# Start of a fused adaLN, attention and GEGLU kernel: scales of the first chain on VectorE, second half's LayerNorm tiles on GpSimd

## The chip, the cores and the metric

The kernel runs on one core of one Trainium2 chip. The metric is the device time of one execution in microseconds (us). Engines are named as in the profile: PE is TensorE (PEld its weight loads), DVE is VectorE, ACT is ScalarE, POOL is GpSimd, SP is SyncE, whose queue issues nearly all transfers.

## The reference

One block of a transformer on 2048 tokens of width 512, in f32. All shift, scale and gate columns come from one small product of `silu(c)` with `w_mod`.

```python
mod = (_silu(c) @ w_mod).reshape(c.shape[0], 6, 1, -1)
sa, ca, ga, sb, cb, gb = (mod[:, 0], mod[:, 1], mod[:, 2], mod[:, 3], mod[:, 4], mod[:, 5])
h = _layernorm(x, axis=-1) * (1 + ca) + sa
x = x + ga * _A_ref(h, A_k_cache, A_v_cache, A_wq, A_wo)
h = _layernorm(x, axis=-1) * (1 + cb) + sb
x = x + gb * _B_ref(h, B_w_gate, B_w_up, B_w_down)
...
# _A_ref: 32 query heads on 8 key/value heads of 128, over the last 512 positions of the cache
q = (x @ wq)
scores = jnp.einsum("bhqd,bhkd->bhqk", q, k) * (Dh ** -0.5)
p = _softmax(scores, axis=-1)
o = jnp.einsum("bhqk,bhkd->bhqd", p, v)
...
# _B_ref
return (_gelu(x @ w_gate) * (x @ w_up)) @ w_down
```

## The kernel before, in words

Every large product is made of three f16 products: each f32 operand is scaled and split into a high half (rounded to f16) and a low half (the rest), and high times high, high times low and low times high are summed in PSUM. The scales keep the halves within f16's range; they are bounds worked out on the chip from norms and maxima (`wsc` for wq, `ksc` for k, `qsc` for q, `ma` for the normalised input; `kmax` and `lw` are norms, `lu`, `lt`, `lr` steps between). Later query projections and the feed-forward part use seven products in the place of eight.

Tokens go in blocks of 512 (four tiles of 128 rows, `QT`), two blocks to a half. The main loop counts steps `t`: each step makes the scores `ps` of one 128-row tile for one head, their maximum `nm` (DVE, `peak`), the exponential `ee` (ACT, `expo`), the probabilities `p` in two halves (ACT and DVE), a transpose of them by DMA (`pt`), and takes a few groups of other matmuls from a list (projections `pq`, `po`, `py`). The order on every engine is written out by hand: functions put under `at(key, ...)` run at that step, and each engine executes its instructions strictly in that order. A wait of one instruction holds back all behind it on its engine.

`begin()` is what runs ahead of step 0. This is the part that the change rewrites:

- The first four x tiles are normalised (`na`): statistics on DVE, the power -1/2 on POOL, the normalisation `xn` on DVE (tiles 0 and 1) and on ACT (tiles 2 and 3).
- The shift column `cols[:,0]` is made by 32 recorded f32 matmuls (`early_cols`, tile `mps`, L1031); the scale column `cols[:,1]` by four multiply-and-sum passes on DVE (`mod_col`, L138). `mod_scale` takes the larger of both over all partitions (`mm`, turned by PE into `pst`, reduced to `mg`) and scales the columns.
- `ln_out(qb, dt)` makes the 512 columns of block `qb` for one quarter `dt` of the width. `turn` transposes four tiles on PE into `pln`; `affine` applies scale and shift to an f32 copy `hf`, which is also stored to DRAM; `direct` does the same to the high half (tile `b` in the profile); `low` subtracts the two.
- `high_w`, `low_w` split wq (`w`), `k0[3]` splits k, `q_first` makes the first query projection `pq`, and `q_post` splits that into `qt`. `warm` and `fill` are matmuls on dummy data.

The second block's four tiles (`nb`, rows 512 to 1023, tile `xb` in the profile) have their statistics and normalisation in steps 0 to 2. Tile 0 goes through ACT (`centre`, `scale`), tiles 1 to 3 through DVE:

```python
at(0, nb[0][2], nb[0][3], nb[1][0], nb[1][1], nb[2][0], nb[2][1])
at(1, nb[1][2], nb[3][0], nb[3][1], nb[2][2])
...
at(2, nb[3][2], *[o[0] for o in o1])
```

The transposes of `xb` (`o1[dt][0]`) stand in PE's order behind the scores of step 2 and ahead of those of step 3: tiles 0 and 1, four `fill`, tile 2, four `fill`, tile 3 and with it the 12 transposes of the other three quarters.

Of the kernel before, what the change touches and what calls it, by code (L numbers as in the profile page):

```python
# [18 lines left out]
P = 128  # L19
# [46 lines left out]
def block_kernel(ctx: ExitStack, tc: tile.TileContext, x, kT, v, wq, wo, wg, wu, wd, cT, wc, wm, out):  # L66
# [47 lines left out]
    nc.gpsimd.memset(nhalf, -0.5)  # L114
    half_ = const.tile([P, 1], F32, name="half_")
    nc.gpsimd.memset(half_, 0.5)
    ones = const.tile([P, 1], BF16, name="ones")
    nc.gpsimd.memset(ones, 1.0)
    junk = const.tile([P, 512], F16, name="junk")
# [59 lines left out]
    def col(name, i=0):  # L179
        return ST[name][:, i:i + 1]  # L180
# [10 lines left out]
    def absmax(out, src):  # L191
        nc.vector.tensor_reduce(out, src, axis=AX.X, op=ALU.max, apply_absolute_value=True)

    def everywhere(out, m, n, fold=True):
        ps = bank("acc", "pst", NACC)
        for i in range(n):
            nc.tensor.transpose(ps[:, i * P:(i + 1) * P], m[:, i:i + 1].to_broadcast([P, P]), ident)
        src = ps[:, :n * P] if fold else ps[:, :n * P].rearrange("p (n q) -> p n q", n=n)
        nc.vector.tensor_reduce(out, src, axis=AX.X, op=ALU.max)
# [3 lines left out]
        absmax(m, cols[:, j:j + 2, :])  # L203
        return m

    def mod_scale(j, name, const_, m=None, mid=nop, between=nop):
        m, g, s = m or mod_max(j), little("mg", 2, 1), little("ms", 1, 1)
        everywhere(g, m, 2, False)
        mid()
        nc.vector.tensor_tensor(s, g[:, 0:1], g[:, 1:2], op=ALU.add)  # L210
# [10 lines left out]
    def sums(m, n):  # L221
        ps = bank("acc", "pst", NACC)
        nc.tensor.matmul(ps[:, 0:n], ones.to_broadcast([P, P]), m[:, 0:n], start=True, stop=True)
        return ps

# [179 lines left out]
    def ln_first(i, act=False):  # L405
        st = {}

        def norm():
            if i < QT:
                xn[i] = tmp("xn")  # L410
                nc.vector.tensor_scalar(xn[i], acc[i], st["mv"][:, 0:1], st["rs"], op0=ALU.subtract, op1=ALU.mult)
            else:
                xn[i] = xn["b"][:, i - QT, :]
                nc.vector.tensor_scalar(xn[i], acc[i], st["mv"][:, 0:1], st["rs"], op0=ALU.subtract, op1=ALU.mult)

        def centre():
            if i < QT:
                xn[i] = tmp("xn")
            else:
                xn["b"] = pool.tile([P, QT, 512], F32, tag="pt", name="xb", bufs=NPT)  # L420
                xn[i] = xn["b"][:, 0, :]
            nc.scalar.activation(xn[i], acc[i], AF.Identity, bias=st["nm"], scale=1.0)

        def scale():
            nc.scalar.activation(xn[i], xn[i], AF.Copy, scale=st["rs"])

        pre = (lambda: ln_stat(acc[i], st, act), lambda: ln_power(st))
        return pre + ((centre, scale) if act else (norm,))

    def ln_out(qb, dt):  # L430
# [1 line left out]
        p = dt % 2  # L432
        st = {}

        def turn():
            st["ps"] = bank("acc", "pln", NACC)
            for i in range(QT):
                if qb and dt == 0 and i > 1:
                    fill(4)
                nc.tensor.transpose(st["ps"][:, i * P:(i + 1) * P], xn[qb * QT + i][:, dt * P:(dt + 1) * P], ident)  # L440
# [9 lines left out]
        def direct():  # L450
            nc.scalar.activation(block(0, name)[:, p, :], st["ps"], AF.Identity, scale=cols[:, 1, dt:dt + 1], bias=cols[:, 0, dt:dt + 1])

        def low(eng=nc.vector):
            t = block(0, name)
# [569 lines left out]
    wct = [pool.tile([P, 4, 512], F32, tag="pt", name="wct", bufs=NPT) for _ in range(2)]  # L1024

    def early_load(j, dt):
        dma(wct[j][:, dt, :], wc[1, :, dt, :] if j else wm[0, dt])

    def early_cols(ps, dt, w=None):
        for kt in range(KT):  # L1030
# [19 lines left out]

    gps = {}
    na = [ln_first(i, i >= 2) for i in range(QT)]
    nb = [ln_first(QT + i, i == 0) for i in range(QT)]
    o0 = [ln_out(0, dt) for dt in range(KT)]
    SET[0] = [get_w(0), get_w(1)]

# [5 lines left out]

    def q_first(warm):
        ps = bank("acc", "pq", NACC)
        for term, (a, b) in enumerate(((0, 0), (1, 0), (0, 2))):
            for kt in range(KT):
                w, m, p = SET[0][0], BK[0, ("b11", "b21")[kt // 2]], kt % 2
                nc.tensor.matmul(ps, w[:, a, kt * P:(kt + 1) * P], m[:, b + p, :], start=term + kt == 0, stop=term == 2 and kt == KT - 1)
            if term == 0:
                warm(3)  # L1070
        q_post(0, ps)

    def begin():
        now[0] = -1
        for i in range(QT):
            na[i][0]()
            na[i][1]()
        na[2][2]()
        na[3][2]()
        na[0][2]()  # L1080
        na[1][2]()
        na[2][3]()
        na[3][3]()
        block(0, "y")
        for name in ("b11", "b21", "b22", "t3", "t2", "t4", "t1"):
            block(0, name)
        mps = bank("s", "mps", 2)
        wps = bank("s", "warm", 2)

        def warm(n):  # L1090
            for _ in range(n):
                nc.tensor.matmul(wps, junk[:, 0:P], junk, start=True, stop=True)

        for dt in range(KT):
# [5 lines left out]
        pair_stat(0, m, 1)  # L1100
        k0[1]()
        ts(cols[:, 1, :], cols[:, 1, :], 1.0, None, ALU.add)
        ts(cols[:, 0, :], mps[:, 0:KT], 1.0, None, ALU.mult)
        pst = {}

        def mid():
            o0[0][0]()
            pst["w"] = sums(m["m"], 2)
            o0[1][0]()
            pst["k"] = sums(k0[4]["m"], 1)  # L1110
            o0[2][0]()
            o0[3][0]()

        mod_scale(0, "ma", SCALE * TOP13 * TOP13, mod_max(0), mid)
        w = w_first(m["m"], pst["w"])
        o0[0][1](False)
        inv_k = k0[2](False, pst["k"])
        nc.vector.reciprocal(col("wsc", 0), w)
        inv_t, last = w_spread(0, m["m"], w)
        o0[0][3]()  # L1120
        high_w(0)
        for n in range(1, KT):
            o0[n][1](False)
            o0[n][3]()
            if n == 1:
                o0[0][2](nc.gpsimd)
            if n == 2:
                inv_k()
                inv_t()
                last()  # L1130
        warm(4)
        low_w(0)
        o0[1][2]()
        o0[2][2](nc.gpsimd)
# [708 lines left out]
```

## Time and profile before

| what | value |
|---|---|
| median of 3 runs | 1729.52 us (1729.38 to 1730.45) |
| the profiled execution: own time, span of its instructions | 1731.43 us, 1729.6 us |
| busy share of the span: PE, DVE, ACT, POOL | 99%, 82%, 73%, 63% |
| PE busy from 100 to 120 us | 20.00 of 20.00 us |
| PE busy from 0 to 10, 10 to 20, 20 to 24 us | 4.84, 8.86, 2.91 us |
| first maximum of scores (`nm`) begins | 26.06 us |

The profiled execution took 1.9 us longer than the median of the timed runs, and its span is 1.8 us shorter than its own time. Times in the views count from the start of the span; in a row of the timeline the first number is the start, the second the duration (for `x4`, of the four together), and the square bracket gives the idle time ahead of it on its engine and what ended that.

### The profile page before, as it was taken

Reading aid. Unit: us, or ns where it says so; the run is one execution under the profiler, and the core shown is the slowest. Engines: PE = TensorE matmul, PEld = TensorE weight load, DVE = VectorE, ACT = ScalarE, POOL = GpSimd, SP = SyncE. Lnnn points to the kernel's source line nnn. Section 1 sums busy time; section 2 is a strip of 40 time slices with the busy share of each in tenths; the row PEclk is TensorE's granted clock in tenths of the full one; section 3 lists DMA queues with packets and bytes.
Section 4 is the critical chain, followed back from the end, with each engine's and each line's share of the span. In section 5 each row is a group of like instructions: output and inputs, shape, how many; then the busy total and the mean of one; then the engine's idle time right before and its main releaser. Section 6 shows DMA issues by size and latency. Waiting matters only on the chain.

```text
span 1729.6 us, 26339 instructions
## 1 busy us (share of the span) xinstructions
PE 1709.0 (99%) x8012; PEld 786.6 (45%) x8012; DVE 1426.7 (82%) x2476; ACT 1254.7 (73%) x2819; POOL 1090.0 (63%) x1328
## 2 busy tenths in 40 slices
PE   7999999999999999999999999999999999999999
PEld 5444444444444444444444444444444444444444
DVE  7888898888889899888788888888896788676666
ACT  6988788888888877888777877787785354455442
POOL 4879778777788984655665755757760345735424
PEclk9999999999999999999999999999999999999999
DMA  7999999999999998999999999999997556365353
GB/s 235 222 206 209 215 215 204 225 205 219 210 231 218 210 208 183 212 209 228 202 228 214 215 230 209 203 219 225 218 230 166 157 153 195 120 164 174 96 160 102
DMA packets 693454, 343.51 MB, mean 199 GB/s; under 512 B 579136, under 2 KB 602688, under 8 KB 693312
## 3 DMA queue, kind: packets, MB, share of 16 engines
q1 hardware_dynamic: 693024, 341.30, 85.7%
q8 instruction: 63, 1.03, 0.2%
q14 instruction: 79, 0.65, 0.1%
q10 hardware_dynamic: 288, 0.52, 0.1%
HBM read 137.50 MB, written 63.70 MB: 116 GB/s over the span
## 4 chain that ended last, share of the span: by engine, by line
PE 88%; DVE 4%; ACT 3%; DMA 2%; POOL 1%; issue 1%; SPq 0%; POOLq 0%; ACTq 0%; DVEq 0%
PE py L91 19%; PE po L91 17%; PE ps L91 17%; PE fa L91 8%; PE qa L91 8%; PE fc L91 4%; PE qc L91 4%; PE ya L91 3%; PE fb L91 2%; PE qb L91 2%; PE yc L91 2%; DMA pt<-p 1%; DVE p L1016 1%; ACT ee L999 1%; DVE nm L990 1%
## 5 line engine op out<-in xcount | busy, mean ns | idle before, releaser
L999 ACT ACTIVATE ee<-ps,nm 128x512 f32<-128x512 f32 x512 | 349.7, 683 | 185.6 <-DVE nm L990 180.3
L1016 DVE SCALAR_TENSOR_TENSOR p<-ee,rr,p 128x512 f16<-128x512 f32 x512 | 458.3, 895 | 8.1 <-ACT p L1011 7.6
L990 DVE TENSOR_REDUCE nm<-ps 128x1 f32<-128x512 f32 x512 | 350.3, 684 | 97.5 <-PE ps L91 95.2
L91 PE MATMUL ps<-k,qt 128*128 128x512 f16 x1536 | 414.9, 379 | 4.9 <-ACT ee L999 3.5
L1011 ACT ACTIVATE p<-ee,rr 128x512 f16<-128x512 f32 x512 | 364.0, 711 | 20.1 <-DVE rr L1007 11.3
L91 PE MATMUL po<-pt,v 128*128 128x512 f16 x1536 | 372.9, 379 | 2.6 <-DMA pt<-p 0.9
L91 PE MATMUL py<-wo,ot 128*128 128x512 f16 x1536 | 371.3, 379 | 0.0
L91 PEld LDWEIGHTS <-w 128*128 128x128 f16 x2184 | 213.5, 98 | 258.6 <-issue 0.9
L91 PEld LDWEIGHTS <-v 128*128 128x128 f16 x1536 | 150.0, 98 | 184.8 <-issue 2.8
L91 PEld LDWEIGHTS <-ot 128*128 128x128 f16 x1536 | 150.3, 98 | 181.3
L91 PEld LDWEIGHTS <-qt 128*128 128x128 f16 x1536 | 145.7, 98 | 176.4 <-issue 4.6
L1320 POOL TENSOR_TENSOR fg<-fg 128x512 f32<-128x512 f32 x48 | 62.9, 1310 | 134.6 <-DVE fg L1294 131.8
L748 DVE SCALAR_TENSOR_TENSOR ot<-po,ot 128x512 f16<-128x512 f32 x128 | 87.9, 687 | 39.2 <-ACT ot L747 38.7
L1304 ACT ACTIVATE at<-fg 128x512 f16<-128x512 f32 x92 | 56.3, 625 | 80.2 <-DVE fg L1294 60.7
L999 ACT ACTIVATION_READ_ACCUMULATOR ee<-ps,nm 128x1 f32 x512 | 100.1, 196 | 0.0
L960 DVE SCALAR_TENSOR_TENSOR acc<-py,ysc,acc 128x512 f32<-128x512 f32 x128 | 94.7, 740 | 5.3 <-PE py L91 5.3
L91 PE MATMUL qa<-t,w 128*128 128x512 f16 x348 | 84.9, 379 | 0.0
L236 POOL TENSOR_TENSOR lw<-lw,half__86 128x1 f32<-128x1 f32 x39 | 24.9, 639 | 94.7 <-DVE lw L186 94.6
L91 PE MATMUL fa<-t,w 128*128 128x512 f16 x336 | 81.6, 379 | 0.1
L747 ACT ACTIVATE ot<-po 128x512 f16<-128x512 f32 x128 | 73.9, 577 | 5.0 <-PE po L91 5.0
L403 POOL TENSOR_TENSOR rs<-rs,nhalf 128x1 f32<-128x1 f32 x32 | 18.7, 584 | 92.7 <-DVE rs L397 89.7
L91 PEld LDWEIGHTS <-wo 128*128 128x128 f16 x504 | 49.3, 98 | 59.6 <-issue 0.3
(243 smaller groups left out, 2813.8 us busy)
## 6 DMA issues: line engine op xcount, KB each, us to landing
w<-kept SPq DMA_DIRECT2D x123, 256.0 KB, 3.3
wo<-kept SPq DMA_DIRECT2D x72, 256.0 KB, 3.3
kept<-stage SPq DMA_DIRECT2D x67, 256.0 KB, 3.0
raw<-in_wo SPq DMA_DIRECT2D x56, 256.0 KB, 3.2
kept<-w SPq DMA_DIRECT2D x39, 256.0 KB, 3.4
rw<-in_wq SPq DMA_DIRECT2D x38, 256.0 KB, 3.1
hs<-hf SPq DMA_DIRECT2D x32, 256.0 KB, 2.7
pt<-p SPq DMA_TRANSPOSE x512, 3.5
```

The lines of the kernel that those rows point to most:

```text
L91: nc.tensor.matmul(ps, a, b, start=first and n == 0, stop=last and n == 2, skip_group_check=chain)
L236: nc.gpsimd.tensor_tensor(out, out, half_, op=ALU.pow)
L403: nc.gpsimd.tensor_tensor(st["rs"], st["rs"], nhalf, op=ALU.pow)
L747: nc.scalar.activation(t[:, 0, :], src, AF.Copy, scale=scale)
L748: return lambda: nc.vector.scalar_tensor_tensor(t[:, 1, :], src, scale, t[:, 0, :], op0=ALU.mult, op1=ALU.subtract)
L960: nc.vector.scalar_tensor_tensor(acc[ti], st["p"], by, acc[ti], op0=ALU.mult, op1=ALU.add)
L990: nc.vector.tensor_reduce(nm, E[t]["ps"], axis=AX.X, op=ALU.max, negate=True)
L999: nc.scalar.activation(e, E[t]["ps"], AF.Exp, bias=E[t]["nm"], scale=1.0, accum_out=sm[:, t % 2:t % 2 + 1])
L1011: nc.scalar.activation(p16[:, 0, :], E[t]["e"], AF.Copy, scale=E[t]["r"])
L1016: nc.vector.scalar_tensor_tensor(p16[:, 1, :], E[t]["e"], E[t]["r"], p16[:, 0, :], op0=ALU.mult, op1=ALU.subtract)
L1304: nc.scalar.activation(t[:, 0, :], g, AF.Copy)
L1320: nc.gpsimd.tensor_tensor(g[o], g[a], g[b], op=ALU.subtract)
```

## The change

It touches only the start: `begin()`, three helpers that it calls, and where the second block's tiles are normalised.

- Shift column: quarters 2 and 3 are made on DVE by `mod_col`, as the scale column is; `early_cols` makes quarters 0 and 1 alone. All 16 transposes of `xn` stand ahead of the first maximum, in place of behind it.
- `mod_scale` has two small DVE instructions fewer ahead of the columns; `ma` is made on POOL.
- The norms of wq and k share one power on POOL (`lk`, two columns), and the steps behind it that were POOL's are DVE's.
- The high halves are made straight after the columns, quarters 0 and 2 on ACT, 1 and 3 on DVE. The f32 copies `hf` follow, all four on ACT. Low halves: quarter 0 on POOL, 1 to 3 on DVE.
- `q_first` does its second term (low half of wq) ahead of the dummy matmuls; `high_w(1)` follows it.
- The statistics of the second block's first tile move from `begin()` to step 0, behind the first `nm`; steps 0 and 1 hold two tiles each, and all four normalisations are POOL's.

```diff
-    def mod_scale(j, name, const_, m=None, mid=nop, between=nop):
+    def mod_scale(j, name, const_, m=None, mid=nop, box=None):
...
-        nc.vector.tensor_tensor(s, g[:, 0:1], g[:, 1:2], op=ALU.add)
-        ts(s, s, FLOOR, RT / TOP13, ALU.max)
-        ts(col(name), s, const_)
-        between()
-        nc.vector.reciprocal(s, s)
-        ts(cols[:, j:j + 2, :], cols[:, j:j + 2, :], s)
+        nc.vector.tensor_scalar(s, g[:, 0:1], g[:, 1:2], FLOOR, op0=ALU.add, op1=ALU.max)
+        inv = little("mi", 1, 1)
+        nc.vector.reciprocal(inv, s)
+        ts(cols[:, j:j + 2, :], cols[:, j:j + 2, :], inv, TOP13 / RT)
+        pool_ts(col(name), s, const_ * RT / TOP13)
...
             else:
+                if i == QT:
+                    xn["b"] = pool.tile([P, QT, 512], F32, tag="pt", name="xb", bufs=NPT)
                 xn[i] = xn["b"][:, i - QT, :]
-                nc.vector.tensor_scalar(xn[i], acc[i], st["mv"][:, 0:1], st["rs"], op0=ALU.subtract, op1=ALU.mult)
+                pool_ts(xn[i], acc[i], st["mv"][:, 0:1], st["rs"], ALU.subtract, ALU.mult)
...
+        for dt in (2, 3):
+            mod_col(0, dt, wct[0][:, dt, :], sbc)
+        for dt in range(2):
+            early_cols(mps, dt)
+        for tiles in ((0, 1), (2, 3)):
+            for dt in range(KT):
+                o0[dt][0](tiles)
         for dt in range(KT):
             mod_col(1, dt, wct[1][:, dt, :], sbc)
-        for dt in range(KT):
-            early_cols(mps, dt)
+            if dt == 1:
+                ts(cols[:, 0, 0:2], mps[:, 0:2], 1.0, None, ALU.mult)
...
+        ts(lk[:, 0:1], sum_w[:, 0:1], TINY, sum_w[:, 1:2], ALU.max, ALU.add)
+        ts(lk[:, 1:2], sum_k, TINY, None, ALU.max)
+        nc.gpsimd.tensor_tensor(lk, lk, half2, op=ALU.pow)
+        warm(6)
+        o0[0][3]()
+        o0[1][3](False)
+        ts(w, lk[:, 0:1], 1.005 / PRE / TOP13)
         nc.vector.reciprocal(col("wsc", 0), w)
...
+        ts(u, w, col("kmax", 0), col("ma"))
+        nc.gpsimd.tensor_tensor(lt, u, half_, op=ALU.pow)
+        o0[2][3]()
+        o0[3][3](False)
         high_w(0)
...
+        for n in range(KT):
+            o0[n][1]()
+        o0[0][2](nc.gpsimd)
         for n in range(1, KT):
...
+            o0[n][2]()
         low_k = k0[3](True)
-        o0[3][2]()
         low_k()
-        nb[0][0]()
-        nb[0][1]()
+        q_first(warm)
         high_w(1)
-        q_first(warm)
...
-    at(0, nb[0][2], nb[0][3], nb[1][0], nb[1][1], nb[2][0], nb[2][1])
-    at(1, nb[1][2], nb[3][0], nb[3][1], nb[2][2])
+    at(0, *nb[0], *nb[1])
+    at(1, *nb[2], *nb[3])
...
-    at(2, nb[3][2], *[o[0] for o in o1])
+    at(2, *[o[0] for o in o1])
```

On POOL, between the last low halves of block 0 and the first low halves of block 1 (`y`), there stand before (`rs` is the power, one for each tile of the second block):

```order
L262 TENSOR_TENSOR lt<-lu,half__86 128x1
L240 TENSOR_SCALAR lt<-lt 128x1
L455 TENSOR_TENSOR b_199<-hf,b_199 128x512
L240 TENSOR_SCALAR qsc<-lt 128x1
L240 TENSOR_SCALAR lr<-lr,lu 128x1
L240 TENSOR_SCALAR ksc<-lr,kinv 128x1
L455 TENSOR_TENSOR b_200<-hf,b_200 128x512
L403 TENSOR_TENSOR rs<-rs,nhalf 128x1 x4
L455 TENSOR_TENSOR y<-hf,y 128x512 x2
```

And now:

```order
L1128 TENSOR_TENSOR lt<-lu,half__86 128x1
L458 TENSOR_TENSOR b_201<-hf,b_201 128x512
L404 TENSOR_TENSOR rs<-rs,nhalf 128x1
L241 TENSOR_SCALAR xb<-acc,mv,rs 128x512
...
L404 TENSOR_TENSOR rs<-rs,nhalf 128x1
L241 TENSOR_SCALAR xb<-acc,mv,rs 128x512
L458 TENSOR_TENSOR y<-hf,y 128x512 x2
```

The small scale steps and one low half left POOL, and power and normalisation now alternate there for the four tiles (the pairs of tiles 1 and 2 are left out above).

On ACT, from the norms of k to the first halves of q, there stand before:

```order
L219 ACTIVATE junk,lm<-raw 128x512
L451 ACTIVATE b_199<-pln,cols 128x512
L1058 ACTIVATE w_150<-rw,wsc 128x512
L451 ACTIVATE b_199<-pln,cols 128x512
L451 ACTIVATE b_200<-pln,cols 128x512 x2
L747 ACTIVATE k<-raw,ksc 128x512
L1058 ACTIVATE w_151<-rw,wsc 128x512
L747 ACTIVATE qt<-pq,qsc 128x512
```

And now:

```order
L220 ACTIVATE junk,lm<-raw 128x512
L452 ACTIVATE b_201<-pln,cols 128x512
L452 ACTIVATE b_202<-pln,cols 128x512
L1061 ACTIVATE w_152<-rw,wsc 128x512
L445 ACTIVATE hf<-pln,cols 128x512 x4
L750 ACTIVATE k<-raw,ksc 128x512
L750 ACTIVATE qt<-pq,qsc 128x512
L1061 ACTIVATE w_153<-rw,wsc 128x512
```

Two high halves went to DVE, four f32 copies came, and the second half of the wq pair moved behind `qt`.

On DVE, from the split of k to the maximum of step 2, there stand before:

```order
L748 SCALAR_TENSOR_TENSOR k<-raw,ksc,k 128x512
L393 BN_STATS bn<-acc 128x6
...
L748 SCALAR_TENSOR_TENSOR qt<-pq,qsc,qt 128x512
L1061 SCALAR_TENSOR_TENSOR w_151<-rw,wsc,w_151 128x512
L990 TENSOR_REDUCE nm<-ps 128x1
...
L990 TENSOR_REDUCE nm<-ps 128x1
L414 TENSOR_SCALAR xb<-acc,mv,rs 128x512
...
L990 TENSOR_REDUCE nm<-ps 128x1
```

And now:

```order
L751 SCALAR_TENSOR_TENSOR k<-raw,ksc,k 128x512
L751 SCALAR_TENSOR_TENSOR qt<-pq,qsc,qt 128x512
L1064 SCALAR_TENSOR_TENSOR w_153<-rw,wsc,w_153 128x512
L993 TENSOR_REDUCE nm<-ps 128x1
L394 BN_STATS bn<-acc 128x6
...
L993 TENSOR_REDUCE nm<-ps 128x1
L394 BN_STATS bn<-acc 128x6
...
L993 TENSOR_REDUCE nm<-ps 128x1
```

The statistics left the place ahead of the first `nm`, and the `xb` rows left DVE. From step 3 on the order is the same on every engine, but for the second use of `mod_scale`, at step 260, which loses two small DVE instructions and gains one on POOL.

More of the change, by code (lines that the diff above doesn't have):

```diff
@@ L116, in block_kernel @@
     nc.gpsimd.memset(half_, 0.5)
+    half2 = const.tile([P, 2], F32, name="half2")
+    nc.gpsimd.memset(half2, 0.5)
     ones = const.tile([P, 1], BF16, name="ones")
@@ L192, in absmax, with everywhere @@
         nc.vector.tensor_reduce(out, src, axis=AX.X, op=ALU.max, apply_absolute_value=True)
-    def everywhere(out, m, n, fold=True):
-        ps = bank("acc", "pst", NACC)
+    def everywhere(out, m, n, fold=True, ps=None):
+        ps = bank("acc", "pst", NACC) if ps is None else ps
         for i in range(n):
@@ L433, in ln_out, with turn @@
         st = {}
-        def turn():
-            st["ps"] = bank("acc", "pln", NACC)
-            for i in range(QT):
+        def turn(tiles=range(QT)):
+            if 0 in tiles:
+                st["ps"] = bank("acc", "pln", NACC)
+            for i in tiles:
                 if qb and dt == 0 and i > 1:
@@ L1052, in block_kernel @@
     na = [ln_first(i, i >= 2) for i in range(QT)]
-    nb = [ln_first(QT + i, i == 0) for i in range(QT)]
+    nb = [ln_first(QT + i) for i in range(QT)]
     o0 = [ln_out(0, dt) for dt in range(KT)]
@@ L1100, in begin @@
         pair_stat(0, m, 1)
+        ts(cols[:, 1, :], cols[:, 1, :], 1.0, None, ALU.add)
+        sum_w, sum_k = pst[:, 256:258], mps[:, 2 * KT:2 * KT + 1]
+        mod_scale(0, "ma", SCALE * TOP13 * TOP13, mod_max(0), lambda: sums(m["m"], 2, sum_w), pst)
         k0[1]()
[L1102 to L1112, printed above, removed]
```

57 lines of the change are left out of this document (24 added, 33 removed).

## The prediction

> **What bounds the kernel now.** I read the page first, for the shares of the whole span, and then the windows, since the change lies in the first 35 of 1730 us.
>
> ```profile
> span 1729.6 us, 26339 instructions
> PE 1709.0 (99%) x8012; PEld 786.6 (45%) x8012; DVE 1426.7 (82%) x2476; ACT 1254.7 (73%) x2819; POOL 1090.0 (63%) x1328
> ```
>
> ```profile
> 28.20:33.09 4.89, 4.32 (x21) 1.84 (x20) 4.70 (x13) 3.47 (x8) 1.51 (x3) 1.00 0.02 5
> 33.09:52.00 18.91, 18.91 (x113) 11.46 (x114) 15.19 (x28) 17.04 (x42) 13.04 (x20) 1.00 1.05 215
> 80.00:90.00 10.00, 7.81 (x36) 3.30 (x35) 8.50 (x15) 9.02 (x23) 9.50 (x9) 1.00 0.85 217
> 100.00:120.00 20.00, 20.00 (x97) 9.07 (x95) 17.88 (x37) 17.21 (x42) 14.46 (x25) 1.00 1.03 212
> ```
>
> In a row of the windows stand the length, then busy time (and instructions) of PE, PEld, DVE, ACT and POOL, the granted clock, the DMA share and GB/s. PE is full from 33.09 to 52 us and from 100 us. In between it pauses at times, but there the other engines are nearly full and hand work to each other. So a change ahead of 33 us is worth what it does to the moment at which the machine gets into this full run, and that moment is read from the timeline.
>
> ```profile
> 26.06 0.68 DVE L990 TENSOR_REDUCE nm<-ps 128x1 f32<-128x512 f32 x1
> 26.66 0.68 DVE L393 BATCH_NORM_STATS2 bn<-acc 128x6 f32<-128x512 f32 x1
> 27.83 0.56 POOL L403 TENSOR_TENSOR rs<-rs,nhalf 128x1 f32<-128x1 f32 x1 [2.42 <-DVE rs L397]
> 32.51 0.53 DVE L414 TENSOR_SCALAR xb<-acc,mv,rs 128x512 f32<-128x512 f32 x1
> 33.09 1.64 PE L440 MATMUL pln<-ident,xb 128*128 128x128 f32 x13 [0.57 <-DVE xb L414]
> 33.46 1.53 DVE L186 TENSOR_SCALAR hf<-pln,cols 128x512 f32<-128x512 f32 x2 [0.42 <-PE pln L440]
> ```
>
> The last `xb` tile ends at 33.04 us, PE starts its 13 transposes at 33.09, and DVE, having waited 0.42 us for them, goes on at 33.46. All later scores stand behind these transposes on PE, and all later work of DVE and ACT behind the `hf` that they give. I call 33.09 the gate. Two spans lead to it: from the start to the first `nm` (26.06 us), and from there to the end of the last `xb` (6.98 us). The change shortens the first and lengthens the second.
>
> **The first span.** These rows carry it.
>
> ```profile
> 6.04 6.83 PE L1031 MATMUL mps<-silu,wct 128*128 128x1 f32 x32
> 8.41 1.00 DVE L411 TENSOR_SCALAR xn<-acc,mv,rs 128x512 f32<-128x512 f32 x2
> 9.64 0.69 DVE L138 SCALAR_TENSOR_TENSOR wct<-wct,sbc 128x512 f32<-128x512 f32 x1 [0.23 <-DMA wct<-in_wc]
> 13.10 0.16 DVE L192 TENSOR_REDUCE mm<-cols 128x2 f32<-128x8 f32 x1
> 14.51 0.16 DVE L210 TENSOR_TENSOR ms<-mg 128x1 f32<-128x1 f32 x1
> 14.70 0.15 DVE L186 TENSOR_SCALAR ms<-ms 128x1 f32<-128x1 f32 x1
> 15.28 0.23 DVE L184 TENSOR_SCALAR cols<-cols,ms 128x8 f32<-128x8 f32 x1
> 17.74 1.44 ACT L451 ACTIVATE b<-pln,cols 128x512 f16<-128x512 f32 x2
> 20.40 1.28 DVE L455 TENSOR_TENSOR b<-hf,b 128x512 f16<-128x512 f32 x2
> 23.89 0.69 ACT L747 ACTIVATE qt<-pq,qsc 128x512 f16<-128x512 f32 x1 [0.42 <-PE pq L1068]
> 25.54 0.39 PE L91 MATMUL ps<-k,qt 128*128 128x512 f16 x1 [0.31 <-DVE qt L748]
> 25.40 0.74 DVE L1061 SCALAR_TENSOR_TENSOR w<-rw,wsc,w 128x512 f16<-128x512 f32 x1
> ```
>
> Step by step:
>
> 1. DVE now makes six column passes in place of four. The first no longer waits for the 0.23 us of DMA, since the columns that come first are loaded earlier, so they start at 9.41. PE's 32 small matmuls become 16 and end near 9.5. Six passes of 0.69 and two small instructions of about 0.2 bring `mm` to 13.9: 0.8 later than 13.10. The 16 transposes of `xn` (3.7 us, below) fit on PE between 9.5 and 13.9.
> 2. From `mm` to the scaled columns it was 15.28 less 13.10, 2.18 us; two dependent small instructions go at 0.19 each (14.51 to 14.70). So 1.8, and the columns begin at 15.7 and are there at 15.93.
> 3. ACT then has seven instructions on 512 columns in a row: two high halves, `w`, four `hf`. At 0.72 (17.74, two in 1.44) they end at 20.95. The scales from POOL (one power for two norms, one for `lt`) come beside this: `wsc` at about 17.2, when ACT is just free for `w`. POOL is not the bound here, and freeing it of its small steps is worth nothing more.
> 4. The last low half on DVE, 0.64 (20.40, two in 1.28), ends at 21.65. The last matmul of `pq` takes 0.39, as the single one at 25.54 does: 22.05. ACT's `qt` takes 0.69, DVE's low half of `qt` and low half of `w` 0.74 each (25.40), with 0.05 us for each hand-over: 24.2. The split of k (ACT at 21, DVE behind the last low half, done by 22.5) and the third score matmul (23.9) lie beside that.
> 5. So the first `nm` begins at 24.2, 1.9 earlier than 26.06. Bounds: an `hf` on ACT has no row; the nearest run from 0.60 to 0.78, which makes 0.5 less or 0.25 more for four. Low half 0 on POOL (1.15 us, row below) may slow DVE's three beside it. I take a gain of 1.9, between 1.0 and 2.5.
>
> ```profile
> L132 ACT ACTIVATE sbc<-sps 128x512 f32<-128x512 f32 x1 | 0.6, 598 | 2.3 <-PE sps L130 2.3
> L451 ACT ACTIVATE b<-pln,cols 128x512 f16<-128x512 f32 x4 | 3.0, 774 | 2.4 <-DVE kmax L184 1.9 <-DVE hf L186 0.6
> L455 POOL TENSOR_TENSOR b<-hf,b 128x512 f16<-128x512 f32 x2 | 2.3, 1154 | 0.0
> L440 PE MATMUL pln<-ident,xn 128*128 128x128 f32 x16 | 3.7, 418 | 0.0
> L414 DVE TENSOR_SCALAR xb<-acc,mv,rs 128x512 f32<-128x512 f32 x3 | 1.6, 533 | 0.0
> ```
>
> **The second span.** What leaves DVE is 3 x 0.53 us of `xb` (the last row above), and ACT's two passes over tile 0. What comes is four normalisations on POOL, and the same instruction (subtract, then multiply, both by a column) runs on POOL eight times later in the kernel:
>
> ```profile
> L240 POOL TENSOR_SCALAR acc<-acc,mv,rs x8: 2064/2082/2520, 688.6 to 769.4; 128x512 f32<-128x512 f32 x8
> L240 POOL TENSOR_SCALAR gs<-gate,osc x8: 687/692/1049, 66.8 to 580.9; 128x512 f32<-128x512 f32 x8
> 713.83 0.55 POOL L403 TENSOR_TENSOR rs<-rs,nhalf 128x1 f32<-128x1 f32 x1 [1.68 <-DVE rs L397]
> 714.38 2.08 POOL L240 TENSOR_SCALAR acc<-acc,mv,rs 128x512 f32<-128x512 f32 x1
> ```
>
> It takes 2.08 us, four times DVE's 0.53, and follows its power without a gap. POOL does power and normalisation tile after tile, so four tiles take 4 x (0.55 + 2.08) = 10.5 us in a row. DVE's statistics take about 1 us each (26.66 to 27.83, POOL's start included, is 1.17) and are never late after the first. From the start of the first `nm` to the first power it was 27.83 less 26.66, 1.17, behind 0.60 for the maximum: 1.8 us. So the last `xb` ends 12.3 us behind the start of the first `nm`, in place of 6.98: 5.3 later. Bounds: with every one at the worst 2.52 it is 1.8 more; below 2.06 no row of this form goes.
>
> Who waits: on PE the transpose of tile 1 holds the four `fill` behind it, tiles 2 and 3 the next, and tile 3 all scores from step 3. DVE's `hf` and ACT's `y` stand behind that. On POOL the low halves of `y` come behind the last `xb`, but they need ACT's `y` anyway, which is later. SP's stores of `hf` and loads behind them shift along with it. The gain of DVE's freed 1.6 us is nothing: it stands idle until the gate.
>
> **Sum.** The gate moves by -1.9 + 5.3 = +3.4 us. Behind it the order is the same and no engine has a backlog that the extra time would work off, so I carry the whole to the end. The rest of the change is nothing: at step 260 `mod_scale` trades 0.4 us on DVE for 0.2 on POOL, inside a stretch where PE is full.
>
> One cost is left, PE's clock. The rows of PE ahead of the gate are these:
>
> ```profile
> 29.45 0.81 PE L91 MATMUL ps<-k,qt 128*128 128x512 f16 x3
> 30.09 0.38 PE L440 MATMUL pln<-ident,xb 128*128 128x128 f32 x2
> 30.31 1.03 PE L1049 MATMUL fill<-ones 128*128 128x512 bf16 x4
> ```
>
> The scores of step 2, done at 30.26 here, are done near 28.4 with the first span 1.9 shorter. The transpose of tile 1 comes at 24.2 + 1.8 + 2 x 2.63 = 31.3, so PE pauses for 2.9 us with one transpose in between, and for about 1.5 us behind each of the two groups of `fill`. What it costs if the array slows down, I bound by the first transposes:
>
> ```profile
> 13.32 0.69 PE L197 MATMUL pst<-ident,mm 128*128 128x128 f32 x2 [0.45 <-DVE mm L192]
> 13.80 1.06 PE L440 MATMUL pln<-ident,xn 128*128 128x128 f32 x4
> 17.36 1.03 PE L1092 MATMUL warm<-junk 128*128 128x512 f16 x4
> 82.39 0.81 PE L91 MATMUL ps<-k,qt 128*128 128x512 f16 x3 [1.86 <-ACT ee L999]
> ```
>
> Four took 1.06 us at 13.80, after a time of light work, where 13 took 1.64 at the gate: about half speed, and some 4 us after PE's start at 13.32 the matmuls at 17.36 ran at full speed (four in 1.03), though the windows show a granted clock of 1.00 throughout. After the 1.86 us pause at 82.39 three took 0.81, no loss. So the cost is between nothing and half of 4 us, 2.0; I take 0.5, as the longest pause, near 3 us, lies between the two cases. The Trainium skill, "TensorE: Matmul & The Clock Gate", section "Part 1: The HAM clock gate (the "warmup" mystery)", says that the array falls to half its clock after an idle window of about 3.4 us and comes back after as long a busy one; by it the cost would be 0 if no window is idle throughout, and an estimated 1.7 us if one is. Nothing in this trace shows the fall itself.
>
> The sum is +3.9. The profiled execution's span would go from 1729.6 to 1733.5 and its own time from 1731.43 to 1735.3; timed runs lie 1.9 below that, so I add 3.9 to the median of 1729.52: 1733.4 us.
>
> **Rivals.**
>
> - *POOL does the normalisation at the speed of its other passes (not slower).* With a single column as factor the same size takes 0.69 (the `gs` row). Then a tile takes 1.24 on POOL, less than two statistics and the maximum between them, the last power begins about 5.5 us behind the first `nm`, the last `xb` ends near 30.9, and the gate is 2.1 earlier: 1727.4 us, within 0.2% of before. It decides from about 1.2 us for one normalisation, where 5.3 later becomes 1.9. Against it: eight rows of the very form, none under 2.06. The Trainium skill, "GPSIMD Engine Reference", section "4.1 Engine selection", says that GpSimd does elementwise work with one input at roughly line rate; the trace agrees for the `gs` row and not for this form, at three times that.
> - *The stretch from 52 to 100 us takes the delay up.* PE pauses there, 2.19 of 10 us in the row from 80 to 90. If the delay only ate such pauses, 2 of the 3.9 us would go: 1731.5. Against it: ACT and POOL are at 9.02 and 9.50 of 10 there, and they are as late as PE.
> - *The clock falls.* The full 2.0, and with it 1735 us; with slower POOL passes beside DVE as well, up to 1736.5.
> - *The first span gains nothing* (ACT's seven in a row wait for more than I see): +5.3 and the 0.5, 1735.3 us.
>
> **How the numbers follow.** 0.2%, about what a measurement of this kernel can tell from no change, is 3.5 us here. Forecast, with its small bounds on both sides: 0.62, of which three in five lie above 3.5. Clock: 0.13. No gain in the first span: 0.06. Taken up later: 0.13. POOL fast: 0.06. So slower is 0.37 + 0.13 + 0.06 = 0.56, faster by over 3.5 us 0.03 out of the last two cases, since even a full gain of the first span with nothing lost is only 2.5, and the rest, 0.41, is within. The range leaves out the fast POOL and the ends of the others: 1731.2 (first span at its best, or part taken up) to 1736.6 us.
>
> **What would show it.** Right: first `nm` near 24.2; four `xb` rows on POOL at 2.1 us; PE's transposes waiting for POOL and starting at 36 to 37; DVE idle for some 5 us ahead of `hf`; everything behind shifted by the same amount up to the end. Wrong: `xb` rows of 0.7 us; a gate ahead of 33; a shift at the gate that is gone by 100 us; or, for the clock, more than 2.5 us for the 13 transposes, where they took 1.64.

## The result, and the profile after

The changed kernel takes 1735.05 us (median of 10 runs, 1733.71 to 1735.5), the kernel before 1730.32 in the same runs (10 runs, 1729.38 to 1732.57). The medians differ by 4.7 us. The ratio over all these runs is 1.0025, with a 95% interval of 1.0016 to 1.0034: slower by 4.3 us, between 2.8 and 5.9. The profiled execution of after took 1734.15 us.

The page of after, its shares of the whole span:

```profile
span 1732.4 us, 26316 instructions
PE 1710.0 (99%) x7996; PEld 784.9 (45%) x7998; DVE 1426.6 (82%) x2477; ACT 1254.7 (72%) x2819; POOL 1097.2 (63%) x1326
```

The shares tell nothing of the change: POOL has 7 us more, and the other engines are within 1 us of before. The timeline of after does, in the rows that answer to those of the prediction (start, duration, engine, line, operation, tiles, and in brackets how long the engine stood idle and for whom):

```profile
13.44 0.16 DVE L194 TENSOR_REDUCE mm<-cols 128x2 f32<-128x8 f32 x1
15.29 0.23 DVE L188 TENSOR_SCALAR cols<-cols,mi 128x8 f32<-128x8 f32 x1
17.73 2.77 ACT L445 ACTIVATE hf<-pln,cols 128x512 f32<-128x512 f32 x4
19.42 2.16 DVE L458 TENSOR_TENSOR b<-hf,b 128x512 f16<-128x512 f32 x3
20.74 1.27 PE L1071 MATMUL pq<-b,w 128*128 128x512 f16 x4
24.09 0.68 DVE L993 TENSOR_REDUCE nm<-ps 128x1 f32<-128x512 f32 x1
25.92 0.55 POOL L404 TENSOR_TENSOR rs<-rs,nhalf 128x1 f32<-128x1 f32 x1 [6.10 <-DVE rs L398]
26.59 2.08 POOL L241 TENSOR_SCALAR xb<-acc,mv,rs 128x512 f32<-128x512 f32 x1
29.32 2.08 POOL L241 TENSOR_SCALAR xb<-acc,mv,rs 128x512 f32<-128x512 f32 x1
34.74 2.08 POOL L241 TENSOR_SCALAR xb<-acc,mv,rs 128x512 f32<-128x512 f32 x1
36.87 2.75 PE L440 MATMUL pln<-ident,xb 128*128 128x128 f32 x13 [0.53 <-POOL xb L241]
37.38 1.67 DVE L188 TENSOR_SCALAR hf<-pln,cols 128x512 f32<-128x512 f32 x2 [6.66 <-PE pln L440]
40.31 0.69 DVE L993 TENSOR_REDUCE nm<-ps 128x1 f32<-128x512 f32 x1 [1.26 <-PE pst L224]
```

The first `nm` comes at 24.09, 1.97 earlier than before. Then four tiles go through POOL, one every 2.71 to 2.73 us, the last `xb` ends at 36.82, and the gate opens at 36.87, 3.78 later than the 33.09 of before. DVE had waited 6.66 us for it. The 13 transposes take 2.75 in place of 1.64, and the maximum of step 3 is at 40.31. The windows of after, with the columns as in the prediction, show PE's clock in this stretch:

```profile
28.00:32.00 4.00, 1.12 (x5) 0.50 (x5) 2.60 (x8) 2.38 (x7) 3.81 (x4) 1.00 0.07 25
32.00:36.00 4.00, 2.63 (x8) 0.77 (x6) 0.00 (x0) 0.00 (x0) 3.87 (x3) 0.55 0.02 4
36.00:40.00 4.00, 3.47 (x17) 2.88 (x17) 1.62 (x2) 1.55 (x2) 1.73 (x2) 0.60 0.19 71
100.00:120.00 20.00, 20.00 (x97) 8.83 (x96) 17.59 (x35) 18.54 (x47) 12.17 (x17) 1.00 1.08 238
```

Between 32 and 36 us DVE and ACT do nothing at all and POOL works 3.87 of 4 us. PE's granted clock is 0.55 there and 0.60 in the next four.

How far the delay is carried is read from the same maximum in both timelines, at steps 3, 32, 192 and 224. Before:

```profile
35.41 0.69 DVE L990 TENSOR_REDUCE nm<-ps 128x1 f32<-128x512 f32 x1 [0.43 <-PE pst L223]
104.00 0.69 DVE L990 TENSOR_REDUCE nm<-ps 128x1 f32<-128x512 f32 x1 [0.64 <-PE ps L91]
510.45 0.69 DVE L990 TENSOR_REDUCE nm<-ps 128x1 f32<-128x512 f32 x1
592.43 0.69 DVE L990 TENSOR_REDUCE nm<-ps 128x1 f32<-128x512 f32 x1 [0.17 <-PE ps L91]
```

After, from step 32 on (step 3 stands above):

```profile
108.27 0.69 DVE L993 TENSOR_REDUCE nm<-ps 128x1 f32<-128x512 f32 x1 [0.47 <-PE ps L91]
514.72 0.69 DVE L993 TENSOR_REDUCE nm<-ps 128x1 f32<-128x512 f32 x1
595.97 0.68 DVE L993 TENSOR_REDUCE nm<-ps 128x1 f32<-128x512 f32 x1
```

The shift is 4.90 us at step 3, 4.27 at step 32 and still 4.27 at step 192. At step 224 it is 3.54, and the spans differ by 2.8. This later loss is of the size by which executions of the same code differ: from step 192 to step 224 the profiled execution of before took 81.98 us and that of after 81.25, but e7 and e9 (below), whose code is the same up to there, took 81.96 and 81.16. Two profiled executions of the same after (the second one below) stand 1.05 us apart at step 192 and 0.1 at the end. The timed runs, with 2.8 to 5.9, are too wide to choose between these shifts.

### The profile page after: what moved, and what is told of

It is laid out like the page before. It is cut to its first block, busy times and chain, and to the rows that moved or that the text cites. A ratio compares the mean times of both kernels' runs of the same rounds, so it can differ in the third digit from the quotient of the medians.

```text
span 1732.4 us, 26316 instructions
## 1 busy us (share of the span) xinstructions
PE 1710.0 (99%) x7996; PEld 784.9 (45%) x7998; DVE 1426.6 (82%) x2477; ACT 1254.7 (72%) x2819; POOL 1097.2 (63%) x1326
## 4 chain that ended last, share of the span: by engine, by line
PE 92%; DVE 3%; ACT 3%; issue 1%; DMA 1%; POOL 1%; POOLq 0%; DVEq 0%; ACTq 0%
PE py L91 20%; PE ps L91 18%; PE po L91 18%; PE qa L91 8%; PE fa L91 8%; PE fc L91 4%; PE qc L91 4%; PE ya L91 3%; PE fb L91 2%; PE qb L91 2%; PE yc L91 2%; PE pq L91 1%; PE yb L91 1%; ACT ee L1002 1%; ACT p L1014 1%
```

## The experiments

Eleven kernels were run against the kernel before. Gate and shift are of each one's profiled execution (33.09 before), the shift being that of the maximum of step 3 (35.41 before) and of step 192 (510.45). Each ratio is to runs of before made beside that kernel; their median was 1730.3 to 1731.0, so medians of two rows may differ by some tenths of a us for that alone.

| kernel | median us | ratio to before, 95% | gate | shift, step 3 | shift, step 192 |
|---|---|---|---|---|---|
| after | 1735.05 | 1.0025 [1.0016, 1.0034] | 36.87 | +4.90 | +4.27 |
| after again | 1735.72 | 1.0028 [1.0018, 1.0038] | 36.88 | +3.79 | +3.22 |
| e1 first chain alone | 1729.13 | 0.9990 [0.9981, 0.9999] | 31.53 | -1.56 | -1.48 |
| e2 GpSimd part alone | 1737.4 | 1.0038 [1.0025, 1.0050] | 39.01 | +7.37 | +6.94 |
| e3 PE kept busy | 1734.91 | 1.0021 [1.0012, 1.0030] | 38.17 | +5.08 | +4.76 |
| e4 multiply only | 1728.65 | 0.9987 [0.9978, 0.9995] | 31.02 | -2.07 | -2.29 |
| e5 two passes | 1738.96 | 1.0046 [1.0033, 1.0059] | 39.02 | +7.39 | +7.20 |
| e6 ACT and DVE | 1729.67 | 0.9995 [0.9986, 1.0004] | 31.99 | -1.16 | -1.41 |
| e7 add negated mean | 1729.13 | 0.9992 [0.9984, 1.0001] | 31.30 | -1.79 | -1.90 |
| e8 multiply, then add | 1730.09 | 0.9996 [0.9987, 1.0005] | 32.62 | -0.46 | -0.56 |
| e9 late ones too | 1728.22 | 0.9986 [0.9977, 0.9994] | 31.22 | -1.87 | -2.16 |
| e10 last tile on DVE | 1729.85 | 0.9991 [0.9982, 1.0000] | 33.28 | +0.14 | -0.21 |

**The two halves of the change, each alone.** e1 is after with the second span of before:

```
-                pool_ts(xn[i], acc[i], st["mv"][:, 0:1], st["rs"], ALU.subtract, ALU.mult)
+                nc.vector.tensor_scalar(xn[i], acc[i], st["mv"][:, 0:1], st["rs"], op0=ALU.subtract, op1=ALU.mult)
...
+        nb[0][0]()
+        nb[0][1]()
         q_first(warm)
...
-    at(0, *nb[0], *nb[1])
-    at(1, *nb[2], *nb[3])
+    at(0, nb[0][2], nb[0][3], nb[1][0], nb[1][1], nb[2][0], nb[2][1])
+    at(1, nb[1][2], nb[3][0], nb[3][1], nb[2][2])
...
-    at(2, *[o[0] for o in o1])
+    at(2, nb[3][2], *[o[0] for o in o1])
```

> The first part of the change alone: the second block's tiles are normalised as before (tile 0 on ACT, 1 to 3 on DVE, statistics of tile 0 ahead of the first maximum). Theory (POOL's four normalisations set the gate, and each microsecond at the gate goes to the end): first nm near 24.3, gate (PE's 13 transposes) near 31.2, 1.9 earlier than before, transposes in 1.6 us, time 1.5 to 2 us below before. Rival (the new first chain itself costs time, or what it gains is lost again ahead of the full stretch): gate at 31 to 33 but time as before or above.

e2 is the reverse: before with after's second span (the same lines with the signs turned, in before).

> The second part alone: the first chain as before, the second block's four tiles on POOL with their statistics behind the first maximum. Theory: first nm near 25.9, the last xb 12.8 us behind it, gate near 38.7, 5.6 later than before; PE's clock falls as in the changed kernel, the 13 transposes take about 2.7 us; time 6 to 7 us above before. Rival (the POOL part is hidden beside other work, and the loss comes from the first chain): gate within 1 us of before, time within 1 us of before.

In the timeline of e1 the first maximum is at 24.48 and the gate at 31.53; in that of e2 they are at 26.29 and 39.01:

```profile
24.48 0.69 DVE L995 TENSOR_REDUCE nm<-ps 128x1 f32<-128x512 f32 x1
31.53 1.64 PE L442 MATMUL pln<-ident,xb 128*128 128x128 f32 x13 [0.58 <-DVE xb L415]
```

```profile
26.29 0.68 DVE L988 TENSOR_REDUCE nm<-ps 128x1 f32<-128x512 f32 x1
39.01 3.03 PE L438 MATMUL pln<-ident,xb 128*128 128x128 f32 x13 [0.53 <-POOL xb L240]
```

So the first chain alone gives a gain, 1.6 us at step 3 and 1.7 at the end (0.2 to 3.3). The GpSimd part alone costs 7.4 at step 3 and 6.6 at the end (4.3 to 8.7). Together that is +5.8 at step 3, where after shows 4.9 and 3.8. At the gate the two make -1.56 + 5.92 = +4.4, where after shows +3.8. Of this difference of 0.6, 0.36 stood already at `mm` in e2 (13.46 for 13.10), which has there the code of before. What else differs at step 3 is the stretch from the gate to that maximum: 2.32 in before, e1 and the second execution of after, 3.44 in the first, 3.77 in e2; that is PE's clock, below. Within this the two spans add up as the prediction has it.

e1 also shows that 0.4 of the 1.97 by which after's first maximum is earlier is due to the second part of the change: with tile 0's statistics ahead of it, the first maximum of e1 is at 24.48 and not 24.09.

**Why is the normalisation slow on GpSimd?** The prediction took 2.08 us from rows of the same form, and saw a single column take 0.69. e4 leaves the mean out of the normalisation, with one column:

```
-                pool_ts(xn[i], acc[i], st["mv"][:, 0:1], st["rs"], ALU.subtract, ALU.mult)
+                pool_ts(xn[i], acc[i], st["rs"])
```

> The changed kernel with the four POOL normalisations reduced to a multiplication by one column; the mean is not subtracted, so that part of the LayerNorm is left out for the second block. Theory (the form with two columns is what is slow): 0.69 us each, last xb near 30.9, gate near 31, 2 us earlier than before, clock at 1.00, time 1.5 to 2 us below before. Rival (POOL is slow here for the data or for DVE beside it): about 2.08 us each and the changed kernel's time.

e5 does the whole of it in two passes of one column each:

```
-                pool_ts(xn[i], acc[i], st["mv"][:, 0:1], st["rs"], ALU.subtract, ALU.mult)
+                pool_ts(xn[i], acc[i], st["mv"][:, 0:1], 1.0, ALU.subtract)
+                pool_ts(xn[i], xn[i], st["rs"])
```

> The changed kernel with each POOL normalisation in two passes of one column each (subtract the mean, then multiply). Theory: 0.69 us each, 1.4 for a tile in place of 2.08, last xb near 33.6, gate near 33.7, 0.6 later than before; time 0.3 to 1.7 us above before, the higher with a fall of the clock. Rival (subtraction is the slow part): first pass near 1.5 to 2 us, second 0.69, gate at the changed kernel's or later.

The groups of `xb` in e4, and then in e5 (shortest, median and longest in ns, first and last start):

```profile
L241 POOL TENSOR_SCALAR xb<-acc,rs x4: 695/695/698, 26.3 to 30.3; 128x512 f32<-128x512 f32 x4
```

```profile
L241 POOL TENSOR_SCALAR xb<-acc,mv x4: 2003/2004/2010, 26.2 to 36.2; 128x512 f32<-128x512 f32 x4
L241 POOL TENSOR_SCALAR xb<-xb,rs x4: 697/698/698, 28.3 to 38.3; 128x512 f32<-128x512 f32 x4
```

One column is not fast as such: the pass that subtracts takes 2.00 us with a single column, the one that multiplies 0.70. My theory that the second column makes the instruction slow fell; the slow part is the subtraction. VectorE beside it isn't the cause: the last `xb` of after runs while VectorE does nothing and takes the same 2.08. Nor is a column of a wider tile, as the mean is one, slow as such: `osc` is one too, and `gs` takes 0.69 with it in the prediction's row. With 2.00 + 0.70 a tile takes longer than in after, and the gate comes at 39.02.

e7 then does the whole normalisation, two columns in one instruction, without a subtraction; VectorE makes the negated mean:

```
-                pool_ts(xn[i], acc[i], st["mv"][:, 0:1], st["rs"], ALU.subtract, ALU.mult)
+                pool_ts(xn[i], acc[i], st["nm"], st["rs"], ALU.add, ALU.mult)
...
-        return pre + ((centre, scale) if act else (norm,))
+        return pre + ((centre, scale) if act and i < QT else (norm,))
...
-    nb = [ln_first(QT + i) for i in range(QT)]
+    nb = [ln_first(QT + i, True) for i in range(QT)]
```

> The changed kernel, whole, but GpSimd's normalisation of the second half's tiles adds the negated mean and multiplies by rs, two columns in one instruction as before, without a subtraction (VectorE makes the negated mean, one small instruction of about 0.15 us per tile). Theory A (GpSimd's subtraction is what is slow; multiplication is fast): whether addition is slow as the subtraction is or fast as the multiplication, no row shows. If addition is fast: xb near 0.7 to 0.75 us, gate near 31.2, step 3's maximum about 2 us ahead of the kernel before, 1728.5 to 1729. If addition belongs with the subtraction: xb 2.0 to 2.1 us, gate 37 to 38, near 1735. Theory B (subtraction alone is special because of the order of its operands): fast.

e8 turns the order round, with one more small instruction on GpSimd per tile:

```
-                pool_ts(xn[i], acc[i], st["mv"][:, 0:1], st["rs"], ALU.subtract, ALU.mult)
+                pool_ts(xn[i], acc[i], st["rs"], st["nr"], ALU.mult, ALU.add)
+
+        def power():
+            ln_power(st)
+            if i >= QT:
+                st["nr"] = small.tile([P, 1], F32, name="nmean")
+                nc.gpsimd.tensor_scalar(st["nr"], st["mv"][:, 0:1], st["rs"], -1.0, op0=ALU.mult, op1=ALU.mult)
...
-        pre = (lambda: ln_stat(acc[i], st, act), lambda: ln_power(st))
+        pre = (lambda: ln_stat(acc[i], st, act), power)
```

> The changed kernel, whole, but GpSimd multiplies by rs and then adds the column -mean*rs, made by one more small GpSimd instruction per tile (about 0.3 us). The same two operations as in the run with the negated mean, in the other order. Theory (the cost lies in the operation, whichever place it has): the same xb duration as in that run within 0.1 us; with a fast addition gate near 31.5 and 1728.5 to 1729.3, with a slow one gate 37 to 38.5 and about 1735.5. Rival (the cost lies in the first operation alone, a multiplication first is fast whatever follows): xb 0.7 here even if the run with the negated mean shows 2.0.

The groups and the gates of e7, then of e8:

```profile
L241 POOL TENSOR_SCALAR xb<-acc,nmean,rs x4: 766/769/772, 26.3 to 30.5; 128x512 f32<-128x512 f32 x4
31.30 1.64 PE L440 MATMUL pln<-ident,xb 128*128 128x128 f32 x13 [0.18 <-POOL xb L241]
```

```profile
L241 POOL TENSOR_SCALAR xb<-acc,rs,nmean x4: 766/766/767, 26.5 to 31.8; 128x512 f32<-128x512 f32 x4
32.62 1.64 PE L446 MATMUL pln<-ident,xb 128*128 128x128 f32 x13 [0.55 <-POOL xb L241]
```

0.77 us for two columns, in either order. With a column as operand, multiplication and addition are fast and subtraction is slow. GpSimd isn't slow at subtracting as such: the low halves of `b` subtract one whole tile from another of the same size there, and the prediction's row has 1.15 us for one, little over half of the 2.00. With that the gate of e7 is 5.57 us ahead of after's, and the whole loss is gone: the interval of e7 ends at 1.0001, that of after begins at 1.0016. For e8 I had the gate at 31.5 and it came at 32.62: the small instruction (0.27 us and its hand-over) stands in the series four times, and all of it shows at the gate. Its median is 1 us over e7's, near the 1.3 of the gate, but by their intervals the two are not told apart.

**Without GpSimd, on the other engines.** e6 normalises two tiles on ACT in one pass each (bias -mean·rs made on GpSimd) in step 1 and two on DVE in step 2:

```
-                pool_ts(xn[i], acc[i], st["mv"][:, 0:1], st["rs"], ALU.subtract, ALU.mult)
+                if i < QT + 2:
+                    nc.scalar.activation(xn[i], acc[i], AF.Identity, bias=st["nr"], scale=st["rs"])
+                else:
+                    nc.vector.tensor_scalar(xn[i], acc[i], st["mv"][:, 0:1], st["rs"], op0=ALU.subtract, op1=ALU.mult)
...
-    at(0, *nb[0], *nb[1])
-    at(1, *nb[2], *nb[3])
+    at(0, *nb[0][:2], *nb[1][:2])
+    at(1, nb[0][2], nb[1][2], *nb[2][:2], *nb[3][:2])
...
-    at(2, *[o[0] for o in o1])
+    at(2, nb[2][2], nb[3][2], *[o[0] for o in o1])
```

> A version meant to beat both: the new first chain, statistics behind the first maximum as in the change, but tiles 0 and 1 normalised on ACT in one pass (scale and bias from POOL), 2 and 3 on DVE. Theory: last xb near 31.7, gate near 31.8, 1.3 earlier than before, no fall of the clock, time 1 to 1.5 us below before. Rival (ACT's two passes hold up the exponential of step 2 and DVE's two the maximum): gate near 33, time as before.

The gate is at 31.99 and the ratio 0.9995: no better than e7, and not told from before.

**PE's clock.** e3 is after with matmuls on a constant filling PE's waits ahead of the transposes of tiles 1 to 3:

```
-                if qb and dt == 0 and i > 1:
-                    fill(4)
+                if qb and dt == 0 and i > 0:
+                    fill((0, 10, 11, 11)[i])
```

> The changed kernel with more dummy matmuls on PE while it waits for the second block's tiles (10, 11 and 11 ahead of tiles 1, 2 and 3, in place of 0, 4 and 4). Theory (pauses let the clock fall): granted clock 1.00 throughout from 28 us, gate still near 36.9, 13 transposes in 1.6 us instead of 2.75, the maximum of step 3 near 39.2 instead of 40.3, time 1.1 us below the changed kernel. Rival (the transposes are slow because POOL and PE meet at the data, or for another reason that pauses have no part in): transposes stay near 2.7, time as the changed kernel.

And after was run once more, unchanged, beside it:

> The changed kernel once more, on the same chip as the three beside it. Theory: gate at 36.9 again, clock near 0.6 of full from 32 to 40 us, time 4 to 5 us above before. Rival (the clock fell by chance in the one profiled execution): clock at 1.00, maximum of step 3 near 39.2.

The rows of e3 at its first matmuls of q and at the gate:

```profile
18.17 3.62 PE L1071 MATMUL pq<-b,w 128*128 128x512 f16 x8
21.58 0.86 PE L1095 MATMUL warm<-junk 128*128 128x512 f16 x3
38.17 1.64 PE L440 MATMUL pln<-ident,xb 128*128 128x128 f32 x13
```

The windows of after's second profiled execution:

```profile
20.00:24.00 4.00, 2.74 (x10) 0.66 (x8) 3.48 (x6) 3.03 (x6) 0.00 (x0) 1.00 1.01 277
24.00:28.00 4.00, 3.76 (x10) 1.35 (x11) 2.78 (x9) 0.78 (x2) 1.95 (x2) 0.59 1.01 364
36.00:40.00 4.00, 3.12 (x22) 2.27 (x23) 2.33 (x4) 1.57 (x3) 1.87 (x2) 1.00 0.26 98
```

With PE kept busy the transposes take 1.64 and the granted clock is 1.00 from 20 us on. From the first maximum to that of step 3 it is 15.10 us, 16.22 in after. But the same 15.10 stand in the second execution of the unchanged after, where the clock had fallen at 24 to 28, on the way to the gate that POOL sets anyway, and cost nothing there (gate 36.88 against 36.87). So the rival of that run, a fall by chance, came true for the gate: its clock is 1.00 there and its maximum of step 3 at 39.20. In e3, in turn, the eight matmuls at 18.17 ran at 0.45 each and the speed of 0.29 came only at 21.58; in after, eight took 2.25 from 18.00. That made its first maximum 1.3 later. So the clock costs from nothing to 1.5 us (e2 and e5, with 3.03 for the transposes), depending on when it changes in that execution. One profiled execution is a single draw: that of e3 is the slowest of its 11 runs, the second one of after the fastest of its 8. Over the timed runs, filling the waits brought nothing that can be told: 1.0021 against 1.0025 and 1.0028.

**Better versions.** e9 is e7 with the addition in the eight later normalisations too (`return pool_ts(st["x"], st["x"], st["nm"], st["rs"], ALU.add, ALU.mult)`, the negated mean made on VectorE there too).

> The run with the negated mean, and in the eight normalisations on GpSimd between 688 and 770 us the addition of the negated mean in place of the subtraction as well (2.08 us each in every run so far). They would take 0.77 us each, 10.5 us of GpSimd's time in all. Theory (the subtraction cost time at the start only since the gate waited for it; PE is full from 100 us and GpSimd is idle for nearly half of that stretch, 10.7 of 20 us busy): the end moves by nothing that can be measured, 1728.5 to 1729.6. Rival (the slow passes hold up GpSimd's own queue, weights and low halves among them, and so PE there too): 1 to 3 us less, 1726 to 1728.

e10 is e7 with the last tile on VectorE, its power ahead of the third tile's normalisation:

```
-                pool_ts(xn[i], acc[i], st["nm"], st["rs"], ALU.add, ALU.mult)
+                if i < QT + 3:
+                    pool_ts(xn[i], acc[i], st["nm"], st["rs"], ALU.add, ALU.mult)
+                else:
+                    nc.vector.tensor_scalar(xn[i], acc[i], st["mv"][:, 0:1], st["rs"], op0=ALU.subtract, op1=ALU.mult)
...
-    at(1, *nb[2], *nb[3])
+    at(1, *nb[2][:2], *nb[3][:2], nb[2][2])
...
-    at(2, *[o[0] for o in o1])
+    at(2, nb[3][2], *[o[0] for o in o1])
```

> The run with the negated mean, but the last of the four tiles is normalised by VectorE (subtract, multiply, 0.53 us), its power made ahead of the third tile's normalisation on GpSimd. Theory (the gate is GpSimd's series of powers and normalisations, and the gate's time is carried to the end less some half a microsecond): last xb near 30.4 in place of 31.24, gate near 30.5, step 3's maximum near 32.8, about 0.8 us less: 1728.0 to 1728.6. Rival (the gate has come to PE's own work or VectorE's maxima now, as the maximum of step 2 at 29.3 lies close by): nothing gained, 1728.9 to 1729.5.

The late group in e9, then the windows and the gate of e10:

```profile
L241 POOL TENSOR_SCALAR acc<-acc,nmean,rs x8: 768/980/1307, 687.3 to 765.8; 128x512 f32<-128x512 f32 x8
```

```profile
24.00:28.00 4.00, 3.78 (x10) 1.42 (x11) 2.76 (x10) 0.78 (x2) 1.86 (x4) 0.57 1.01 345
33.28 1.58 PE L443 MATMUL pln<-ident,xb 128*128 128x128 f32 x13
```

e9 beats both kernels: 1728.22 us, 2.4 less than before (1.0 to 4.0). At step 3 it is 1.87 ahead of before, and e1, with the first chain alone, 1.56: most of the gain is the first chain's. The late additions took 0.98 (0.77 to 1.31) where I had expected 0.77; the subtractions in their place take 2.07 to 2.53 in e7. Whether they add to the gain stays open: e9's median is 0.9 below e7's, but the intervals overlap, and of the 2.4 us between their profiled spans 1.06 stood there at step 224 (590 us), ahead of the late normalisations. e10 is inconclusive: its profiled execution had the clock fall at 24 to 28, in code that does not differ from e7's up to there. The scores of steps 1 and 2 came late, statistics and powers behind them, and the gate with them. So its 33.28 doesn't test the order of the tiles, and its time is not told from e7's.

## Why the prediction was right, point by point

- **The whole: +3.9 forecast.** The timed runs show 4.3 (4.7 between the medians), and 1735.05 lies inside the range of 1731.2 to 1736.6. The parts that made it in the first execution are 3.78 at the gate, 1.12 for the clock and 0.63 taken up again, which makes 4.27; in the second 3.79, nothing and 0.57, which makes 3.22. That the sum with 0.5 for the clock and nothing taken up came so near is in part luck, as the two misses work against each other.
- **First span: right.** The first `nm` came at 24.09 where 24.2 was forecast, a gain of 1.97 for 1.9 (0.4 of it, as e1 shows, since tile 0's statistics no longer stand ahead of it; the forecast has them gone as well). Step by step `mm` was 0.46 earlier than forecast (13.44 for 13.9) and the columns 0.41; ACT's `hf` ended at 20.50 for 20.95, at 0.69 each, inside the bounds of 0.60 to 0.78. The lead was lost on DVE: three low halves at 0.72 beside POOL's ended at 21.58 for 21.65, and `pq` at 22.01 for 22.05. DVE's low halves set the end, not ACT's seven in a row. That the first span has a worth of its own is shown by e1.
- **Second span: right in its mechanism, 0.45 short.** Four `xb` at 2.08 as forecast. The last one ended 12.73 behind the start of the first `nm`, for 12.3: power, normalisation and the hand-overs between them take 2.71 a tile, not 2.63. I had read "follows its power without a gap" from one row; here the gap is 0.12 behind a power.
- **The gate:** +3.78 for +3.4, the sum of these two. PE, DVE and ACT stood waiting as described.
- **Clock: the mis-sized term.** I took 0.5 within 0 to 2.0. The transposes took 2.75, over the 2.5 named as its sign, which is 1.1, in the first execution; nothing at the gate in the second. The bound held for after, the way to it did not: the length of PE's pauses alone doesn't decide it, since the clock fell at different moments of the same program.
- **Carried to the end: nearly.** 0.63 of 4.90 was taken up by 104 us, and 0.57 of 3.79 in the second execution; between 104 and 510 us nothing more. The prediction put this at nothing; which engine works it off no run shows. The rival that had 2 of 3.9 taken up there was a third of its size. In the table all kernels carry their shift at step 3 on to step 192 within 0.65.
- **The rivals.** That POOL is fast did not happen, but its price was near: with 0.70 (e4) and 0.77 (e7) the gate comes 2.07 and 1.79 earlier than before, where 2.1 was worked out. For e4 two misses cancel: its first maximum is 0.35 earlier than forecast, and its last `xb` ends 7.1 behind that, not 6.7. "The first span gains nothing" is refuted by e1. What the prediction hadn't separated is what makes the form slow: it named the single column as the difference between 2.08 and 0.69, and e5 and e7 show that it is the subtraction. The sum needed only the row of the same form, and so it stood.

## What to carry to other kernels

Price a moved operation by a row of the very same form on the very same engine: neither the engine's general speed nor the number of operands but the operation, in this form with a column, made the factor of three here. Where such a row is dear, try the same arithmetic in another form (the negated mean added, in place of the mean subtracted) before giving up the move. A series of steps on one engine that the rest waits for counts every small instruction and hand-over in full, and what it shifted here, at a point where all engines wait, was still there for the most part 470 us later.

## What the runs showed of the hardware

- On GpSimd, a pass over 128x512 f32 with column operands takes 0.70 us if it multiplies, 0.77 if it adds and multiplies in either order, 2.00 if it subtracts and 2.08 if it subtracts and multiplies. VectorE takes 0.53 for the last. Why subtraction of a column is slow no run shows; a subtraction of two tiles takes 1.15. The Trainium skill, "GPSIMD Engine Reference", section "4.1 Engine selection", has elementwise add, mul and max with one input at roughly line rate. The runs here agree for multiplication and addition, at 0.70 and 0.77; subtraction, which that row doesn't name, takes 2.6 times as long as the latter.
- PE's time at the lower clock came in lengths of about 3.4 us or a multiple of it. The lower clock is half: e2 has 0.50 from 36 to 40 us. Between 32 and 40 us of after, (1 - 0.55) and (1 - 0.60) times 4 us, doubled for that reason, make 6.8 us at half speed; e2 has 6.8 as well (0.90, 0.50 and 0.75 from 32 to 44 us), e5 10.2 (0.98, 0.50, 0.50 and 0.74 from 28 to 44 us), the second execution of after 3.3 at 24 to 28 us (0.59), and e10 3.4 (0.57). The Trainium skill, "TensorE: Matmul & The Clock Gate", section "Part 1: The HAM clock gate (the "warmup" mystery)", gives a free-running window of about 3.4 us, and the lengths agree, as does the moment that differs from execution to execution. That it takes an idle window to fall does not agree: in the second execution of after PE was busy for 2.74 of the 4 us ahead of the fall. e7 has the same code up to there, with 2.50 of 4 us busy, and its clock did not fall; what decides is not settled.

The windows of e7 for this, and then those of e2:

```profile
20.00:24.00 4.00, 2.50 (x10) 0.54 (x9) 3.48 (x7) 2.75 (x6) 0.00 (x0) 1.00 1.00 278
24.00:28.00 4.00, 4.00 (x19) 1.79 (x19) 3.83 (x12) 1.50 (x4) 2.11 (x4) 1.00 1.00 335
```

```profile
32.00:36.00 4.00, 1.15 (x4) 0.45 (x5) 0.92 (x3) 1.45 (x3) 3.90 (x3) 0.90 0.00 0
36.00:40.00 4.00, 3.17 (x10) 1.66 (x11) 0.48 (x1) 0.00 (x0) 2.85 (x3) 0.50 0.00 0
40.00:44.00 4.00, 4.00 (x21) 2.82 (x20) 2.36 (x4) 2.05 (x3) 2.27 (x2) 0.75 0.55 182
```
